# Strassen's algorithm for the output projection of a gated spatial mix, with its operand sums on GpSimd

## The chip, the core and the metric

The kernel runs on one core of a Trainium2 chip. The time is the device time of one execution in microseconds (us). The kernel before took 309.96 us (median of three runs, 309.31 to 311.14). One more execution was recorded by the hardware profiler. Names of engines: PE is TensorE (matmul), PEld its weight load, DVE VectorE, ACT ScalarE, POOL GpSimd, SP SyncE, whose queue starts nearly all DMAs here.

## The reference, cut to what matters

```python
def _B_ref(x, w_in, w_sp, b_sp, w_out):          # x: 2048 x 640
    Fh = F // 2                                  # 864
    z = _gelu(jnp.einsum('bsd,df->bsf', x, w_in))
    z1 = z[..., :Fh].copy()
    z2 = _layernorm(z[..., Fh:], axis=-1)
    g = jnp.einsum('ts,bsf->btf', w_sp, z2) + b_sp[None, :, None]    # the mix
    return jnp.einsum('bsf,fd->bsd', z1 * g, w_out)                  # the projection
...
    x = x + ga * _A_ref(h, A_k, A_v, A_shift_k, A_ssm_k, A_ssm_D)
    h = _layernorm(x, axis=-1) * (1 + cb) + sb
    x = x + gb * _B_ref(h, B_w_in, B_w_sp, B_b_sp, B_w_out)
    return x
```

Everything ahead of the mix (a long convolution by Fourier transform, layer norms, the first projection) is the same in both kernels. The change concerns the last lines: `u = z1 * g` (2048 x 864) times `w_out` (864 x 640), scaled by `gb` and added to `x`.

## The kernel before, in words

The 2048 rows are 16 tiles of 128. Tile t and tile t + 8 make pair p = t, with p from 0 to 7. The mix (2048 x 2048 times 2048 x 864) is already done by Strassen's algorithm in Winograd's form, over 2 x 2 blocks. For each pair it makes seven products, `product(p, 1)` to `product(p, 7)`. Each is 8 matmuls of 128x128 weights with 432 columns (line 1013). Its sums of `w_sp` blocks (`s_sum`, line 988) and its sums of results (`c11`, `partial`, `c22`, `last_sum`: lines 1030, 1035, 1039 to 1041, 1046 and 1047) are done by DVE. Two results are copied by ACT (`keep`, lines 1019 and 1021). The finished u of a tile is turned by a DMA on SP's queue (`turn_u`, line 1052, into the tile `uT`).

`project(t)` (line 1131) multiplies the turned tile by `w_o`, which is `w_out` times `gb`. It takes two halves of 320 output columns, each summed over seven row tiles of `w_o` (six of 128 rows and one of 96). That is 14 matmuls of 320 columns (line 1137) for a tile and 28 for a pair. DVE adds `xt` to each half (line 1139), and one DMA per tile writes the output (line 1143).

The work up to pair 0 is set by a written list. From pair 1 on a plain loop writes the order. One turn of this loop is called a pass below, and pass p makes the mix's products of pair p in the order 1, 5, 2, 6, 7, 3, 4. Tile p - 1 is projected between products 3 and 4, tile p + 7 after product 4. Pass 7 projects nothing: pairs 6 and 7 are projected behind the loop. Every engine takes its instructions in the order written. Behind product 4 SP's queue gets two loads of `w_sp` (`load_w`, line 974, in passes 1 to 4) ahead of the pair's second `turn_u`. [...]

Of the kernel before, what the change touches and what calls it, by code (L numbers as in the profile page):

```python
# [10 lines left out]
ALU = mybir.AluOpType  # L11
BF16 = mybir.dt.bfloat16
F32 = mybir.dt.float32
I32 = mybir.dt.int32

P = 128
# [19 lines left out]
SLOTS = dict(Tf=2, W=2, X=3, X1=4, KH=9, T=3, Z=3, ZT=1, wm=1, big=2, dg=2, st1=2, s1=1, sm=2, pu=2, pz=2)  # L36
# [93 lines left out]
def kernel(  # L130
# [20 lines left out]
    nc = tc.nc  # L151
    _, S, D = A_q.shape
# [3 lines left out]
    NT = S // P  # L156
    ND = D // P
    NFT = (Fh + P - 1) // P
    fsz = [min(P, Fh - i * P) for i in range(NFT)]
# [3 lines left out]
    HS = D // NH  # L163

    x_nat = A_q[0].rearrange("(n p) d -> p n d", p=P)
    out_nat = out[0].rearrange("(n p) d -> p n d", p=P)
# [9 lines left out]
    bigp = ctx.enter_context(tc.tile_pool(name="bigp", bufs=2))  # L176

    xt = persist.tile([P, NT, D], BF16)
# [14 lines left out]
    span = ctx.enter_context(tc.tile_pool(name="span", bufs=1))  # L193
# [17 lines left out]
    with ExitStack() as pctx:  # L211
# [17 lines left out]
        sums = consta.tile([P, NT, 2], F32)  # L229
# [6 lines left out]
        op = plan.op  # L236
# [549 lines left out]
        for i in range(NKC // KCH):  # L786
# [4 lines left out]
           w=["sc"])  # L791
# [165 lines left out]
        HT = NT // 2  # L957
        wTs, uTs, Ss, part, us, T = {}, {}, {}, {}, [], {}
# [13 lines left out]
        def load_w(t):  # L972
            wTs[t] = bwork.tile([P, NT, P], BF16, tag="wT", bufs=WB, name="wT")
            nc.sync.dma_start_transpose(wTs[t][:], B_w_sp[t * P:(t + 1) * P, :])

        def zb(s0, n, f):
            return tl["z2_%d" % (s0 // TB)][:, s0 % TB:s0 % TB + n, f * FC:(f + 1) * FC]

        def a_of(p, i, j):
            return wTs[p + HT * i][:, j * HT:(j + 1) * HT, :]  # L980

        def s_sum(p, k):
            if p not in Ss:
                Ss[p] = [bwork.tile([P, HT, P], BF16, tag="S%d" % i, bufs=2, name="S%d" % (i + 1)) for i in range(4)]
            S = Ss[p]
            x, y, o = ((a_of(p, 1, 0), a_of(p, 1, 1), ALU.add), (S[0][:], a_of(p, 0, 0), ALU.subtract),
                       (a_of(p, 0, 0), a_of(p, 1, 0), ALU.subtract), (a_of(p, 0, 1), S[1][:], ALU.subtract))[k]
            nc.vector.tensor_tensor(S[k][:], x, y, op=o)
# [13 lines left out]
        def product(p, m, alloc):  # L1002
            S = Ss.get(p)
            lhs = (a_of(p, 0, 0), a_of(p, 0, 1), S and S[3][:], a_of(p, 1, 1), S and S[0][:], S and S[1][:], S and S[2][:])[m - 1]
            rhs = (lambda s_: zb(s_, 1, 0), lambda s_: zb(HT + s_, 1, 0), lambda s_: zb(HT + s_, 1, 1),
                   lambda s_: T[4][:, s_:s_ + 1, :], lambda s_: T[1][:, s_:s_ + 1, :], lambda s_: T[2][:, s_:s_ + 1, :],
                   lambda s_: zb(s_, 1, 1))[m - 1]
            more = m in (2, 3, 4)
            if not more:
                part[p, BANK[m]] = alloc(BANK[m])  # L1010
            ps = part[p, BANK[m]]
            for s_ in range(HT):
                nc.tensor.matmul(ps[:, :FC], lhsT=lhs[:, s_, :], rhs=rhs(s_), start=(s_ == 0 and not more), stop=(s_ == HT - 1),  # L1013
                                 skip_group_check=more)

        def keep(p, m):
            part[p, m] = bwork.tile([P, FC], F32, tag="m%d" % m, bufs=1, name="m%d" % m)
            if m == 1:
                nc.scalar.copy(part[p, m][:], part[p, BANK[m]][:, :FC])  # L1019
            else:  # L1020
                nc.scalar.activation(part[p, m][:], part[p, BANK[m]][:, :FC], ACT.Identity, bias=T["bcol"][:, p + HT:p + HT + 1], scale=1.0)

        def f32(tag):
            return bwork.tile([P, FC], F32, tag=tag, bufs=1, name=tag)

        def ubuf(p, i):
            return us[2 * (p % 2) + i]

        def c11(p):
            nc.vector.scalar_tensor_tensor(ubuf(p, 0)[:, :FC], part[p, "a"][:, :FC], T["bcol"][:, p:p + 1], z1[p][:, :FC],  # L1030
                                           op0=ALU.add, op1=ALU.mult)

        def partial(p):
            part[p, "s"] = f32("s1")
            nc.vector.tensor_tensor(part[p, "s"][:], part[p, "b"][:, :FC], part[p, 1][:], op=ALU.add)

        def c22(p):
            c_ = f32("c22")
            nc.vector.tensor_tensor(c_[:], part[p, "c"][:, :FC], part[p, "s"][:], op=ALU.add)
            nc.vector.tensor_tensor(c_[:], c_[:], part[p, 5][:], op=ALU.add)  # L1040
            nc.vector.tensor_tensor(ubuf(p, 1)[:, FC:Fh], c_[:], z1[p + HT][:, FC:], op=ALU.mult)

        def last_sum(p, bank, i, f):
            c_, sl = f32("c"), slice(f * FC, (f + 1) * FC)
            t = p + HT * i
            nc.vector.scalar_tensor_tensor(c_[:], part[p, bank][:, :FC], T["bcol"][:, t:t + 1], part[p, "s"][:], op0=ALU.add, op1=ALU.add)
            nc.vector.tensor_tensor(ubuf(p, i)[:, sl], c_[:], z1[t][:, sl], op=ALU.mult)

        def turn_u(p, i):
            t = p + HT * i  # L1050
            uTs[t] = bwork.tile([P, NFT, P], BF16, tag="uT", bufs=UB, name="uT")
            nc.sync.dma_start_transpose(uTs[t][:], ubuf(p, i)[:])
# [33 lines left out]
        def zkeys(h, f):  # L1086
            return [("z2_%d" % h, (i, f)) for i in range(TB)]
# [3 lines left out]
        for k in (1, 2, 3, 4):  # L1091
            for h in range(2):
                lo, hi, name = h, h + 2, "T%d" % k
                r, w = {1: (zkeys(lo, 0) + zkeys(lo, 1), [("T1", h)]), 2: (zkeys(hi, 1) + [("T1", h)], [("T2", h)]),
                        3: (zkeys(hi, 1), zkeys(lo, 1)), 4: (zkeys(hi, 0) + [("T2", h)], [("T4", h)])}[k]
# [3 lines left out]
                     w=w + ([(name, "new")] if fresh else []), new=[(name, slot)] if fresh else [])  # L1099
# [5 lines left out]
        for m in (1, 5, 2, 3, 6, 7, 4):  # L1105
            b = BANK[m]
# [18 lines left out]
    psB = ctx.enter_context(tc.tile_pool(name="psB", bufs=2, space=bass.MemoryType.PSUM, reuse_waits="tile"))  # L1125
    w_o = T["w_o"]

    def bank(b):
        return psB.tile([P, 512], F32, tag="mm", bufs=6, name="ps")

    def project(t, tag="o"):
        ot = bwork.tile([P, D], BF16, tag="ot", bufs=3, name="ot")
        last = t == NT - 1
        for i, (lo, hi) in enumerate(((0, HS), (HS, HS + HS // 2), (HS + HS // 2, D)) if last else ((0, HS), (HS, D))):
            ps = psB.tile([P, 512], F32, tag=tag, bufs={"o": 2, "mm": 6}[tag], name="po")
            for ft in range(NFT):
                nc.tensor.matmul(ps[:, :hi - lo], lhsT=uTs[t][:fsz[ft], ft, :], rhs=w_o[:fsz[ft], ft, lo:hi],  # L1137
                                 start=(ft == 0), stop=(ft == NFT - 1))
            nc.vector.tensor_tensor(ot[:, lo:hi], ps[:, :hi - lo], xt[:, t, lo:hi], op=ALU.add)
            if last:  # L1140
                (nc.scalar if i == 1 else nc.sync).dma_start(out_nat[:, t, lo:hi], ot[:, lo:hi])
        if not last:
            nc.sync.dma_start(out_nat[:, t, :], ot[:])

    load_w(3)
    load_w(3 + HT)
    for p in range(1, HT):
        nxt = p + 1 < HT
        product(p, 1, bank)
        keep(p, 1)  # L1150
        product(p, 5, bank)
        keep(p, 5)
        if nxt:
            s_sum(p + 1, 0)
            s_sum(p + 1, 1)
        product(p, 2, bank)
        c11(p)
        if nxt:
            s_sum(p + 1, 2)
        product(p, 6, bank)  # L1160
        partial(p)
        product(p, 7, bank)
        c22(p)
        product(p, 3, bank)
        last_sum(p, "d", 0, 1)
        turn_u(p, 0)
        if nxt:
            project(p - 1)
        product(p, 4, bank)
        last_sum(p, "c", 1, 0)  # L1170
        if p + 3 < HT:
            load_w(p + 3)
            load_w(p + 3 + HT)
        turn_u(p, 1)
        if nxt:
            project(p - 1 + HT)
            s_sum(p + 1, 3)
    for p in range(HT - 2, HT):
        project(p, "mm")
        project(p + HT, "mm")  # L1180


# [28 lines left out]
```

## Time and profile before

| | |
|---|---|
| median of the runs | 309.96 us (309.31 to 311.14) |
| profiled execution, first to last instruction | 310.4 us |
| PE busy | 295.9 us |
| DVE busy | 254.1 us |
| ACT busy | 160.9 us |
| POOL busy | 116.0 us, none of it in the passes |
| passes 1 to 7 | 205.26 to 299.73 us |
| projection behind the loop | 299.73 to 307.56 us |

No other time of the profiled execution is given than its span, which is 0.4 us above the median of the runs. In the profile's rows the first number is a start or a stretch in us from the first instruction, the second a duration. A group row has the count, the busy time and the mean duration of one instruction. "Idle before" is the time that the engine stood still ahead of an instruction, with the engine that ended the wait behind the arrow. The matmul's own duration is longer than the distance between two matmuls, since they are pipelined. The distance is what counts, and the chain of work gives it.

### The profile page before, as it was taken

Reading aid. Unit: us, or ns where it says so; the run is one execution under the profiler, and the core shown is the slowest. Engines: PE = TensorE matmul, PEld = TensorE weight load, DVE = VectorE, ACT = ScalarE, POOL = GpSimd, SP = SyncE. Lnnn points to the kernel's source line nnn. Section 1 sums busy time; section 2 is a strip of 40 time slices with the busy share of each in tenths; the row PEclk is TensorE's granted clock in tenths of the full one; section 3 lists DMA queues with packets and bytes.
Section 4 is the critical chain, followed back from the end, with each engine's and each line's share of the span. In section 5 each row is a group of like instructions: output and inputs, shape, how many; then the busy total and the mean of one; then the engine's idle time right before and its main releaser. Section 6 shows DMA issues by size and latency. Waiting matters only on the chain.

```text
span 310.4 us, 6397 instructions
## 1 busy us (share of the span) xinstructions
PE 295.9 (95%) x2499; PEld 197.3 (64%) x2506; DVE 254.1 (82%) x515; ACT 160.9 (52%) x288; POOL 116.0 (37%) x148
## 2 busy tenths in 40 slices
PE   7897989989999998989999999999999999999996
PEld 2575778867889998645555555455565656555564
DVE  8798998979998988999895998977676858567474
ACT  6987899978888957447666687140101010010100
POOL 2531878838988999555414612000000000000000
PEclk9999999999999999999999999999999999999999
DMA  8999999998995849405698930073938284840414
GB/s 170 216 227 217 257 310 226 207 203 191 221 226 121 193 95 295 143 2 98 123 159 208 185 36 0 2 123 76 201 82 190 63 176 108 131 102 0 104 30 114
DMA packets 127953, 45.22 MB, mean 146 GB/s; under 512 B 117071, under 2 KB 127156, under 8 KB 127924
## 3 DMA queue, kind: packets, MB, share of 16 engines
q1 hardware_dynamic: 127770, 44.78, 68.3%
q8 instruction: 19, 0.31, 0.4%
q14 instruction: 10, 0.08, 0.1%
q10 hardware_dynamic: 154, 0.05, 0.1%
HBM read 16.11 MB, written 5.24 MB: 69 GB/s over the span
## 4 chain that ended last, share of the span: by engine, by line
PE 37%; DVE 19%; POOL 2%; DMA 2%; issue 1%; ACT 1%; POOLq 1%; DVEq 0%; SPq 0%
PE ps L1013 23%; PE po L1137 10%; DVE stz L926 4%; DVE st L704 3%; DMA Z<-Z 2%; PE pz L1013 1%; DVE Tf L462 1%; PE pu L245 1%; DVE xt L698 1%; DVE X L943 1%; POOL rstd L191 1%; DVE T L998 1%; DVE T L462 1%; DVE mv L829 1%; DVE gh L746 1%
## 5 line engine op out<-in xcount | busy, mean ns | idle before, releaser
L245 PEld LDWEIGHTS <-Z 128*128 128x128 bf16 x320 | 31.2, 98 | 28.0 <-DVE Z L871 1.3
L245 PE MATMUL pu<-X,M 128*128 128x128 bf16 (+1 forms) x480 | 45.7, 237 | 2.5 <-DVE Tf L462 2.1
L245 PEld LDWEIGHTS <-M 128*128 128x128 bf16 x480 | 37.3, 98 | 8.7 <-issue 3.1
L1019 ACT COPY m<-ps 128x432 f32<-128x432 f32 x7 | 3.6, 518 | 72.7 <-PE ps L1013 72.7
L1013 PEld LDWEIGHTS <-S 128*128 128x128 bf16 x256 | 25.0, 98 | 22.9 <-issue 1.3
L476 POOL TENSOR_TENSOR W<-Tf 128x256 bf16<-128x256 f32 x47 | 34.7, 760 | 11.4 <-DVE Tf L462 8.1
L245 PE MATMUL pz<-big,Z 128*128 128x432 bf16 x160 | 33.1, 346 | 0.8 <-DVE Z L871 0.8
L248 ACT CAST X<-s 128x1024 bf16<-128x1024 f32 x31 | 31.9, 1030 | 3.1 <-PE s L245 2.9
L1137 PE MATMUL po<-w_o,uT 128*128 128x320 bf16 (+2 forms) x231 | 32.7, 295 | 0.0
L245 PE MATMUL pu<-big,Z 128*128 128x432 bf16 x160 | 32.5, 346 | 0.0
L462 DVE TENSOR_TENSOR Tf<-pu,KH 128x1024 f32<-128x1024 f32 x25 | 30.3, 1219 | 2.6 <-POOL gh L608 1.1
L1013 PEld LDWEIGHTS <-wT 128*128 128x128 bf16 x192 | 18.7, 98 | 15.2
L1137 PEld LDWEIGHTS <-uT 128*128 128x128 bf16 (+1 forms) x231 | 22.2, 98 | 9.7
L245 PEld LDWEIGHTS <-G 128*128 128x128 bf16 x330 | 24.7, 98 | 2.3 <-issue 0.5
L248 ACT CAST KH<-pu 128x512 bf16<-128x512 f32 x40 | 23.0, 600 | 5.9 <-PE pu L245 5.8
L248 ACT CAST Z<-pz 128x512 bf16<-128x512 f32 x38 | 22.3, 602 | 5.3 <-PE pz L245 5.1
L1013 PE MATMUL ps<-T,S 128*128 128x432 bf16 x112 | 22.7, 346 | 0.0
L1013 PE MATMUL ps<-X,wT 128*128 128x432 bf16 x112 | 22.7, 346 | 0.0
L245 PEld LDWEIGHTS <-X 128*128 128x128 bf16 x288 | 18.1, 97 | 6.4 <-DMA X<-kv_scr 1.6
L1013 PE MATMUL ps<-X,S 128*128 128x432 bf16 x112 | 21.6, 346 | 0.0
L245 PE MATMUL s<-F1bd,X 128*128 128x256 bf16 x128 | 19.2, 272 | 1.5 <-DVE X L400 1.2
L245 PE MATMUL sm<-big,dg 128*128 128x512 bf16 (+3 forms) x73 | 19.9, 379 | 0.5
(181 smaller groups left out, 542.6 us busy)
## 6 DMA issues: line engine op xcount, KB each, us to landing
wm<-in_w_mod_dram SPq DMA_DIRECT2D x6, 800.0 KB, 6.2
xt<-in_A_q_dram SPq DMA_DIRECT2D x4, 640.0 KB, 6.2
out_dram<-ot SPq DMA_DIRECT2D x15, 160.0 KB, 2.1
big<-in_B_w_in_dram SPq DMA_DIRECT2D x2, 1080.0 KB, 9.5
X<-in_A_ssm_k_dram SPq DMA_DIRECT2D x4, 512.0 KB, 5.2
kv_scr<-big SPq DMA_DIRECT2D x4, 512.0 KB, 3.5
X<-kv_scr SPq DMA_DIRECT2D x4, 512.0 KB, 4.7
w_o<-in_B_w_out_dram SPq DMA_DIRECT2D x6, 160.0 KB, 3.1
```

What stands on the lines that cost most here:

```text
L191: nc.gpsimd.tensor_tensor(dst, dst, mhalf[:, 0:dst.shape[1]], op=ALU.pow)
L245: nc.tensor.matmul(o, lhsT=w, rhs=x, start=start, stop=stop)
L248: (e.copy if e is nc.scalar else e.tensor_copy)(dst, src)
L462: e.tensor_tensor(T_[:], (tl[pu] if src is None else tl[src])[:, :, :, None, :].to_broadcast(shape), tl[KH][:, :, None, :, :].to_broadcast ...
L476: e.tensor_tensor(tl[W][:, :, o, :], T_[:, :, 0, o, :], T_[:, :, 1, 1 - o, :], op=ALU.add if o else ALU.subtract)
L698: op("GD" if u < NU - 1 else "D", "res", lambda e: e.tensor_tensor(sl, sl, gl, op=ALU.add), r=[("gh", (u, g))], w=[("xt", (u, n)) for n in ...
L704: op("D", "ln2", lambda e, n=n: e.bn_stats(out=st2[:, n, (0, 0, 0, 1, 2)[u], :], in_=xt[:, n, us[0] * DU:(u + 1) * DU]), r=[("xt", (v, n)) ...
L746: op("D", "yml", lambda e, ghv=ghv, py=py, i0=i0, k=k: e.tensor_tensor(ghv, ghv, tl[py][:, i0:i0 + k], op=ALU.mult), r=[py], w=[("gh", (u, ...
L926: op("D", "stz", lambda e, i=i, n=n, fc=fc: e.bn_stats(out=stz[:, n, fc, :], in_=tl[z2][:, i, fc * FC:(fc + 1) * FC]), r=[(z2, (i, fc))], ...
L1013: nc.tensor.matmul(ps[:, :FC], lhsT=lhs[:, s_, :], rhs=rhs(s_), start=(s_ == 0 and not more), stop=(s_ == HT - 1), skip_group_check=more)
L1019: nc.scalar.copy(part[p, m][:], part[p, BANK[m]][:, :FC])
L1137: nc.tensor.matmul(ps[:, :hi - lo], lhsT=uTs[t][:fsz[ft], ft, :], rhs=w_o[:fsz[ft], ft, lo:hi], start=(ft == 0), stop=(ft == NFT - 1))
```

## The change

The projection of pairs 0 to 6 is done by Strassen's algorithm too (Winograd's form). The blocks are the two tiles of a pair by two groups of three row tiles of `w_o`, and the two halves of 320 columns. Seven products of 3 matmuls take the place of eight. The seventh row tile of `w_o` (96 rows) is left over, and is multiplied in the plain way by 4 further matmuls. So a pair has 25 matmuls of 320 columns. Pair 7 is projected as before.

- `weight_sum` makes four sums of `w_o` blocks once (960 columns each; two on POOL, two on DVE) and a fifth small one on POOL (`V5`).
- `u_sums(p)` makes four sums of the turned tiles of a pair on POOL (384 columns each). They wait for both turned tiles.
- `begin` (6 matmuls) stands between products 3 and 4, `most` (15 matmuls) behind product 4, and `end` (4 matmuls) behind product 5 of the next pass.
- Two results per pair are copied by ACT (lines 1197 and 1199). DVE makes five additions with a PSUM operand (lines 1204, 1210, 1217, 1219, 1224) in place of four. POOL makes four additions of 320 columns per pair in SBUF (lines 1200 and 1205 to 1207).
- The banks are 4 for the mix and 4 for the projection. `vbuf`, `rbuf` and `obuf` lie in slots of earlier tiles.

The core of the diff:

```diff
     def bank(b):
-        return psB.tile([P, 512], F32, tag="mm", bufs=6, name="ps")
+        return psB.tile([P, 512], F32, tag="mm", bufs=4, name="ps")
+
+    def obank():
+        return psB.tile([P, 512], F32, tag="o", bufs=4, name="po")
...
+    def weight_sum(e, k):
+        x, y = ((wo_b(0, 1), wo_b(0, 0)), (wo_b(1, 1), V[0]), (wo_b(1, 1), wo_b(0, 1)), (wo_b(1, 0), V[1]))[k]
+        e.tensor_tensor(V[k], x, y, op=ALU.subtract)
...
+    def u_sums(p):
+        R = [rbuf[:, p % 2, i] for i in range(4)]
+        lo, hi = p, p + HT
+        for k, (x, y, o) in enumerate(((u_of(hi, 0), u_of(hi, 1), ALU.add), (R[0], u_of(lo, 0), ALU.subtract),
+                                       (u_of(lo, 0), u_of(hi, 0), ALU.subtract), (u_of(lo, 1), R[1], ALU.subtract))):
+            nc.gpsimd.tensor_tensor(R[k], x, y, op=o)
+        return R
...
+        def begin():
+            piece(a, U[0, 0], B[0, 0], KT, True, True)
+            nc.scalar.copy(m1, a[:, :HS])
+            piece(d, S_[0], V_[0], KT, True, True)
+            nc.scalar.copy(m5, d[:, :HS])
+            nc.gpsimd.tensor_tensor(m5, m5, x_of(1, 1), op=ALU.add)
+
+        def most():
+            piece(b, S_[1], V_[1], KT, True, True)
+            nc.vector.tensor_tensor(s, b[:, :HS], m1, op=ALU.add)
+            nc.gpsimd.tensor_tensor(s12, s, x_of(0, 1), op=ALU.add)
+            nc.gpsimd.tensor_tensor(s22, s, m5, op=ALU.add)
+            nc.gpsimd.tensor_tensor(s21, s, x_of(1, 0), op=ALU.add)
+            piece(a, U[0, 1], B[1, 0], KT, False, False)
+            piece(a, *rest(lo, 0), False, True)
+            nc.vector.tensor_tensor(ot[0][:, 0:HS], a[:, :HS], x_of(0, 0), op=ALU.add)
+            piece(c_, S_[2], V_[2], KT, True, False)
+            piece(c_, *rest(hi, 1), False, True)
+            piece(d, S_[3], B[1, 1], KT, False, False)
+            piece(d, *rest(lo, 1), False, True)
+
+        def sums():
+            nc.vector.tensor_tensor(ot[0][:, HS:D], d[:, :HS], s12, op=ALU.add)
+            nc.sync.dma_start(out_nat[:, lo, :], ot[0][:])
+            nc.vector.tensor_tensor(ot[1][:, HS:D], c_[:, :HS], s22, op=ALU.add)
+
+        def end():
+            piece(c_, U[1, 1], V_[3], KT, False, False)
+            piece(c_, lambda k: uTs[hi][:fl, NFT - 1, :], lambda k: V5[:fl, :], 1, False, True)
+            nc.vector.tensor_tensor(ot[1][:, 0:HS], c_[:, :HS], s21, op=ALU.add)
+            nc.sync.dma_start(out_nat[:, hi, :], ot[1][:])
+        return begin, most, sums, end
+
     load_w(3)
     load_w(3 + HT)
+    weight_sum(nc.gpsimd, 2)
+    weight_sum(nc.vector, 0)
+    R = u_sums(0)
+    weight_sum(nc.vector, 1)
+    weight_sum(nc.gpsimd, 3)
+    nc.gpsimd.tensor_tensor(V5[:fl, :], w_o[:fl, NFT - 1, 0:HS], w_o[:fl, NFT - 1, HS:D], op=ALU.subtract)
+    end = None
     for p in range(1, HT):
         nxt = p + 1 < HT
         product(p, 1, bank)
         keep(p, 1)
         product(p, 5, bank)
         keep(p, 5)
+        if end:
+            end()
...
         c22(p)
+        begin, most, sums, end = project_pair(p - 1, R)
         product(p, 3, bank)
         last_sum(p, "d", 0, 1)
         turn_u(p, 0)
-        if nxt:
-            project(p - 1)
+        begin()
         product(p, 4, bank)
...
         turn_u(p, 1)
+        most()
         if nxt:
-            project(p - 1 + HT)
             s_sum(p + 1, 3)
-    for p in range(HT - 2, HT):
-        project(p, "mm")
-        project(p + HT, "mm")
+        sums()
+        if nxt:
+            R = u_sums(p)
+    project(HT - 1)
+    end()
+    project(NT - 1)
```

DVE's queue in pass 3, from the last operation on product 3's result to the end of the pass. `S` are the sums of `s_sum`, `u` the finished mix, `ot` the output tile. Before:

```order
L1047 TENSOR_TENSOR u_2790<-c,M_80 128x432
L1139 TENSOR_TENSOR ot<-po,xt 128x320 x2
L1046 SCALAR_TENSOR_TENSOR c<-ps,bcol,s_3737 128x432
L1047 TENSOR_TENSOR u_2791<-c,G_81 128x432
L1139 TENSOR_TENSOR ot<-po,xt 128x320 x2
L988 TENSOR_TENSOR S_3715<-wT,S_3713 128x1024
```

With the change (`O` is `obuf`, the additions' other operand, written by ACT, DVE and POOL):

```order
L1047 TENSOR_TENSOR u_2790<-c,M_80 128x432
L1046 SCALAR_TENSOR_TENSOR c<-ps,bcol,s_3765 128x432
L1047 TENSOR_TENSOR u_2791<-c,G_81 128x432
L1204 TENSOR_TENSOR O<-po,O 128x320
L1210 TENSOR_TENSOR ot<-po,xt 128x320
L988 TENSOR_TENSOR S_3743<-wT,S_3741 128x1024
L1217 TENSOR_TENSOR ot<-po,O 128x320
L1219 TENSOR_TENSOR ot<-po,O 128x320
```

The four output additions, which stood behind the two tiles' matmuls, are now five and all stand behind product 4's sums. L1217 and L1219 take operands that POOL makes from the result of L1204, and everything of the next pass stands behind them.

POOL's queue from the start of pass 1, where it had nothing (`V` are the sums of `w_o`, `R` those of the turned tiles):

```order
L1161 TENSOR_TENSOR V<-w_o 128x960
L1171 TENSOR_TENSOR R<-uT 128x384
L1171 TENSOR_TENSOR R<-R,uT 128x384
L1171 TENSOR_TENSOR R<-uT 128x384
L1171 TENSOR_TENSOR R<-uT,R 128x384
L1161 TENSOR_TENSOR V<-w_o,V 128x960
L1235 TENSOR_TENSOR V<-w_o 96x320
L1200 TENSOR_TENSOR O<-O,xt 128x320
L1205 TENSOR_TENSOR O<-O,xt 128x320
L1206 TENSOR_TENSOR O<-O 128x320
L1207 TENSOR_TENSOR O<-O,xt 128x320
```

All three `V` sums stand ahead of the first pair's L1200. For the later pairs the four `R` and the four `O` sums alternate.

More of the change, by code (lines that the diff above doesn't have):

```diff
@@ L1128, in bank, with project @@
     def bank(b):
-        return psB.tile([P, 512], F32, tag="mm", bufs=6, name="ps")
-    def project(t, tag="o"):
+        return psB.tile([P, 512], F32, tag="mm", bufs=4, name="ps")
+    def obank():
+        return psB.tile([P, 512], F32, tag="o", bufs=4, name="po")
+    def project(t):
         ot = bwork.tile([P, D], BF16, tag="ot", bufs=3, name="ot")
@@ L1134, in project @@
         for i, (lo, hi) in enumerate(((0, HS), (HS, HS + HS // 2), (HS + HS // 2, D)) if last else ((0, HS), (HS, D))):
-            ps = psB.tile([P, 512], F32, tag=tag, bufs={"o": 2, "mm": 6}[tag], name="po")
+            ps = obank()
             for ft in range(NFT):
@@ L1143, in project, with wo_b @@
             nc.sync.dma_start(out_nat[:, t, :], ot[:])
+    KT = NFT // 2
+    fl = fsz[-1]
+    vbuf = bigp.tile([P, (4 * KT + 1) * HS], BF16, tag="big", bufs=SLOTS["big"], name="V")
+    V = [vbuf[:, i * KT * HS:(i + 1) * KT * HS].rearrange("p (k d) -> p k d", d=HS) for i in range(4)]
+    V5 = vbuf[:, 4 * KT * HS:]
+    rbuf = span.tile([P, 2, 4, KT, P], BF16, tag="Z", bufs=SLOTS["Z"], name="R")
+    obuf = span.tile([P, 6, HS], F32, tag="Z", bufs=SLOTS["Z"], name="O")
+    def wo_b(i, j):
+        return w_o[:, i * KT:(i + 1) * KT, j * HS:(j + 1) * HS]
@@ new lines, in weight_sum, with u_of @@
+    def weight_sum(e, k):
+        x, y = ((wo_b(0, 1), wo_b(0, 0)), (wo_b(1, 1), V[0]), (wo_b(1, 1), wo_b(0, 1)), (wo_b(1, 0), V[1]))[k]
+        e.tensor_tensor(V[k], x, y, op=ALU.subtract)
+    def u_of(t, i):
+        return uTs[t][:, i * KT:(i + 1) * KT, :]
+    def u_sums(p):
[5 more added lines that the diff above has]
+        return R
@@ new lines, in rows, with piece, project_pair, rest @@
+    def rows(i):
+        return obuf[:, i]
+    def piece(ps, w, x, n, start, stop, m=P):
+        for k in range(n):
+            nc.tensor.matmul(ps[:, :HS], lhsT=w(k), rhs=x(k), start=start and k == 0, stop=stop and k == n - 1, skip_group_check=True)
+    def project_pair(p, R):
+        lo, hi = p, p + HT
+        U = {(i, j): (lambda k, t=t, j=j: uTs[t][:, j * KT + k, :]) for i, t in ((0, lo), (1, hi)) for j in range(2)}
+        B = {(i, j): (lambda k, i=i, j=j: w_o[:, i * KT + k, j * HS:(j + 1) * HS]) for i in range(2) for j in range(2)}
+        S_ = [lambda k, i=i: R[i][:, k, :] for i in range(4)]
+        V_ = [lambda k, i=i: V[i][:, k, :] for i in range(4)]
+        def rest(t, j):
+            return (lambda k: uTs[t][:fl, NFT - 1, :]), (lambda k: w_o[:fl, NFT - 1, j * HS:(j + 1) * HS]), 1
+        ot = [bwork.tile([P, D], BF16, tag="ot", bufs=3, name="ot") for _ in range(2)]
+        x_of = lambda i, j: xt[:, (lo, hi)[i], j * HS:(j + 1) * HS]
+        m1, m5, s, s12, s21, s22 = (rows(i) for i in range(6))
+        a, d, b, c_ = (obank() for _ in range(4))
+        def begin():
[27 more added lines that the diff above has]
+        return begin, most, sums, end
```

## The prediction

> **What bounds the kernel now.** I read the totals first, then a table of engine time by stretch, then the chain that ended last, then DVE's and the DMA queue's order of time in one pass. The totals, and two stretches of about a pass each (length, busy time and instructions of PE, PEld, DVE, ACT and POOL, the clock, DMA):
>
> ```profile
> PE 295.9 (95%) x2499; PEld 197.3 (64%) x2506; DVE 254.1 (82%) x515; ACT 160.9 (52%) x288; POOL 116.0 (37%) x148
> ...
> 232.00:246.00 14.00, 14.00 (x86) 8.19 (x84) 9.70 (x18) 1.14 (x2) 0.00 (x0) 1.00 0.60 130
> 260.00:274.00 14.00, 14.00 (x86) 8.16 (x85) 9.70 (x18) 1.14 (x2) 0.00 (x0) 1.00 0.72 132
> ```
>
> PE never rests in a pass, at full clock. DVE has 4.3 of 14 us free, ACT nearly all, POOL does nothing. The end of the chain of waits (start, us, what):
>
> ```profile
> 270.35 1.91 PE po L1137 x14
> 272.26 1.46 PE ps L1013 x8
> 273.72 1.91 PE po L1137 x14
> 275.63 8.76 PE ps L1013 x48
> ...
> 289.67 10.22 PE ps L1013 x56
> 299.89 7.67 PE po L1137 x63
> 307.56 0.02 issue
> ```
>
> A mix matmul takes 10.22 / 56 = 0.1825 us, a projection matmul 1.91 / 14 = 0.1364, and a pass 289.67 - 275.63 = 14.04 = 10.22 + 28 x 0.1364. Only PE's count, or a new wait of PE, moves the end.
>
> **What is removed.** Three matmuls per pair, seven pairs: 21 x 0.1364 = **-2.86 us**. The matmuls keep their shape, so they keep their price. An undisturbed pass becomes 10.22 + 25 x 0.1364 = 13.63 us.
>
> **The tail loses cover: +0.55.** The start of product 4 of pass 7, the first turn of pair 7 on SP's queue, and what its DMAs take to land (least, median, most):
>
> ```profile
> 298.27 1.62 PE L1013 MATMUL ps<-T,wT 128*128 128x432 bf16 x8
> ...
> 300.25 2.64 SPq L1052 DMA_TRANSPOSE uT<-u  x2
> ...
> DMA to landing us min/median/max: 2.9/2.9/4.7
> ```
>
> From the end of product 3 (298.27) to the turned tile 7 it is 300.25 + 2.9 - 298.27 = 4.88 us. Before, product 4 and two tiles cover this (1.46 + 28 x 0.1364 = 5.28). Now it is `begin`, product 4 and `most`: 0.82 + 1.46 + 2.05 = 4.33. PE waits 0.55, or 2.35 if this landing is one of the slow ones. Tile 15 needs 1.5 (below) + 2.9 = 4.4 us from the end of product 4 and has `most`, the wait, tile 7 and `end`, 2.05 + 0.55 + 1.91 + 0.55 = 5.06, so it is not late.
>
> **What DVE, ACT and POOL get.** Prices of POOL, DVE and ACT (the first three with least, median and most in ns; then busy us and mean ns):
>
> ```profile
> L476 POOL TENSOR_TENSOR W<-Tf x47: 721/727/967, 29.7 to 120.3; 128x256 bf16<-128x256 f32 x47
> L698 POOL TENSOR_TENSOR xt<-xt,gh x10: 1145/1152/1395, 86.4 to 142.7; 128x512 bf16<-128x512 bf16 x10
> L988 DVE TENSOR_TENSOR S<-wT x16: 629/682/687, 155.1 to 280.6; 128x1024 bf16<-128x1024 bf16 x16
> ...
> L1047 DVE TENSOR_TENSOR u<-c,G 128x432 bf16<-128x432 f32 x9 | 5.5, 608 | 0.3
> L1139 DVE TENSOR_TENSOR ot<-po,xt 128x320 bf16<-128x320 f32 x30 | 14.0, 486 | 3.0 <-PE po L1137 3.0
> L1019 ACT COPY m<-ps 128x432 f32<-128x432 f32 x7 | 3.6, 518 | 72.7 <-PE ps L1013 72.7
> ```
>
> By columns, an `R` sum on POOL (384, bf16) is 1.152 x 384 / 512 = 0.87 us. An `O` sum (320, float) lies between 1.152 x 320 / 512 = 0.72 and 0.727 x 320 / 256 = 0.91. I take 0.9, from the float row. The big `V` sums are 2.17 on POOL and, between DVE's rows, 0.65 on DVE. ACT's two copies (0.4 each) hide in its 12.9 idle us. DVE's fifth addition (0.49) hides in its 4.3 us. The smaller banks cost nothing while DVE keeps within a pass: each is filled once a pass, and its reader runs within 3 us of the product.
>
> POOL's 4 x 0.87 + 4 x 0.9 = 7.1 us a pass would fit too. What speaks against it is how the two engines meet in earlier stages (DVE with POOL, four meetings):
>
> ```profile
> 86.52 1.12 DVE L400 TENSOR_TENSOR X<-X,D_col 128x16 bf16<-128x16 bf16 x1
> 86.39 1.16 POOL L698 TENSOR_TENSOR xt<-xt,gh 128x512 bf16<-128x512 bf16 x1
> ...
> 136.98 0.83 DVE L833 SCALAR_TENSOR_TENSOR nmr<-mv,rstd 128x2 f32<-128x2 f32 x1
> 136.63 1.15 POOL L698 TENSOR_TENSOR xt<-xt,gh 128x512 bf16<-128x512 bf16 x1
> ...
> 125.44 0.42 DVE L698 TENSOR_TENSOR xt<-xt,gh 128x512 bf16<-128x512 bf16 x1
> 125.48 1.40 POOL L698 TENSOR_TENSOR xt<-xt,gh 128x512 bf16<-128x512 bf16 x1 [0.84 <-DVE gh L678]
> ...
> 103.50 1.21 DVE L462 TENSOR_TENSOR T<-pu,KH 128x1024 bf16<-128x1024 f32 x1
> 103.67 1.15 POOL L698 TENSOR_TENSOR xt<-xt,gh 128x512 bf16<-128x512 bf16 x1
> ```
>
> Two tiny DVE operations that start inside a POOL sum end only with it (86.52 + 1.12 = 87.64 against 87.55). In the third, POOL starts second and takes 1.40 in place of 1.15: it ends 1.15 - 0.13 after DVE. In the fourth DVE has one operand in PSUM, and neither is slower. So a DVE operation with both operands in SBUF and a POOL sum **exclude each other**, and the later costs its full length less about 0.14. In a pass eight DVE operations are of this kind: four `s_sum`, L1040, L1041 and two L1047, 4 x 0.68 + 4 x 0.61 = 5.2 us. With POOL's 7.1 that is 12.3 of 13.63 us, in orders fixed by hand.
>
> [...]
>
> **Where PE meets this: `end`.** It adds to the bank that L1219 reads, so it waits for L1219, and that for POOL's second `O` sum. Behind `end` on PE stands the whole pass. *Later pairs.* A row of DVE for what follows product 4, whose last matmul ended at 273.56, and SP's queue in a pass with loads, product 4 ended at 217.39:
>
> ```profile
> 273.76 0.67 DVE L1046 SCALAR_TENSOR_TENSOR c<-ps,bcol,s 128x432 f32<-128x432 f32 x1 [0.85 <-PE ps L1013]
> ...
> 217.39 2.07 PE L1137 MATMUL po<-w_o,uT 128*128 128x320 bf16 x14
> ...
> 217.92 5.10 SPq L974 DMA_TRANSPOSE wT<-in_B_w_sp_dram  x2
> 223.11 1.25 SPq L1052 DMA_TRANSPOSE uT<-u  x1
> ```
>
> From the end of product 4, with DVE punctual: L1046 and L1047 until 1.5, L1204 2.0, POOL's first `O` sum 3.0, DVE's `s_sum` held by it until 3.55, POOL's second `O` sum held by that until 4.3, L1219 until 4.9. PE wants `end` after `most` and two products, 2.05 + 2.92 = 4.97. That is just in time. But DVE is not punctual: the second turned tile lands 223.11 + 2.9 - 217.39 = 8.6 us after product 4 (10.4 at worst), so the four `R` sums, 3.5 us plus waits of 0.5 each, run until 13.6 to 15.5 us. They fall on L1040, L1041 and L1047 of the next pass, each held by up to 0.7, where about 0.5 us is spare ahead of the next L1046. DVE comes 0 to 1.2 us late. A wait in one pass gives the next that much more room. I take 0.35 for each of five pairs: **+1.75** (0 to 3.5).
>
> *The first pair* has POOL's `V` sums ahead too. The start of pass 1, and the scaling of `w_o` on which they wait:
>
> ```profile
> 204.91 1.69 DVE L1077 TENSOR_TENSOR w_o<-w_o,gb_bf 128x640 bf16<-128x640 bf16 x4
> 205.26 1.62 PE L1013 MATMUL ps<-X,wT 128*128 128x432 bf16 x8
> ```
>
> Counted from 205.26, POOL begins at 1.3. Until the second `O` sum it has 2 x 2.17 + 4 x 0.87 + 0.7 + 3 x 0.9 = 11.2 us, done at 12.5 alone. DVE's ten operations of the kind in this time (two `V`, four `s_sum`, four float) each push it by their length less 0.14: 1.3 + 2.7 + 2.4 - 1.4 = 5.0. Done at 17.5, L1219 at 18.1. PE wants `end` at 10.22 + 21 x 0.1364 + 2.92 = 16.0. The wait is 2.1, or none without exclusion, or 3.5 where POOL also waits for DVE's other work. I take **+2.4**.
>
> **Sum:** -2.86 + 0.55 + 1.75 + 2.4 = +1.84 us. On the profiled span, 310.4 becomes 312.2. The median of the runs lies 0.4 below that span: 311.8.
>
> **Rivals.** A measurement here can tell about 0.5% (1.55 us) from no change: under 308.4 is faster, over 311.5 slower.
> - *The sums stay out of PE's way* (17%). DVE and POOL interleave with less loss, L1219 is on time, only the tail waits: 309.96 - 2.86 + 0.55 = 307.7. For it: the slack computed above, and the undisturbed meetings with PSUM operands. Against: the three held meetings.
> - *Only the 16-bit sums exclude* (15%). In the first pair the push falls to 1.3 + 2.7 - 0.8 = 3.2 us, so L1219 ends at 16.3 and the wait is 0.3 to 0.9; later pairs are in time: 309.96 - 2.86 + 0.55 + 0.6 = 308.3 (308.0 to 308.6), on the edge of faster. For it: two of the three held meetings are of 16-bit operands. Against: L833 is not.
> - *SP's queue spreads the delay* (15%), slower still. A late L1047 delays a `turn_u`, behind it in SP's queue the loads (5.1 us), behind them the second turn; then `begin` waits for the `R` sums too. It decides from a landing 8.8 us into a pass (9.7, when `begin` reaches `R`, less one sum), where 6.6 is usual and 8.4 the worst by the rows above. With 1 us for each of the four passes with loads: 315.8.
>
> **Numbers.** The forecast has 53%, of which two thirds lie over 311.5 and the rest within 0.5%. Slower: 0.37 + 0.15 = 0.52. Faster: nearly all of the first rival and half of the second, 0.22. Same: 0.26. The range runs from the first rival, 307.7, to my upper waits, -2.86 + 0.9 + 3.5 + 3.5 = +5.0: 315.0. The forecast alone would be 310.5 to 314.
>
> **What would show it.** Passes: waits of PE behind product 5 (at `end`), released by DVE L1219, largest in pass 2, about half a microsecond in some later passes. `s_sum` and L1040 to L1047 above 0.68 and 0.61 us, POOL sums above 0.9. At product 4 of pass 7 a wait of 0.55 for the turned tile. If PE has no gap before `end`, exclusion does not reach it and the kernel is faster; if gaps stand at `begin`, SP's queue was the cause. A pass of 13.63 us without a gap would show that the removed matmuls were worth their price.

## The result, and the profile after

The changed kernel is slower: 313.36 us against 310.17 us (medians of 14 runs each). The ratio is 1.0085, with a 95% interval of 1.0056 to 1.0113, so about +2.6 us (1.7 to 3.5). One run of the changed kernel, at 316.03 us, counts as slow and is left out of the ratio. The medians lie 3.2 us apart, which is inside the interval. The profiled execution spans 312.4 us, 2.0 more than before. Its pass 1 begins 0.68 us earlier than in the profile before (204.58 against 205.26). The work ahead of pass 1 is the same and scatters by more than that between profiles: in the run with pair 0 in the plain way, where pass 2 began at 217.47, pass 1 began at about 203.4, by an estimate from an undisturbed pass of 14.04 us. So everything below is counted from the start of pass 1.

The totals of the page of the changed kernel, and two stretches (length, busy time and instructions of PE, PEld, DVE, ACT and POOL, the clock, DMA):

```profile
PE 295.8 (95%) x2485; PEld 195.7 (63%) x2485; DVE 271.5 (87%) x524; ACT 167.1 (53%) x302; POOL 177.1 (57%) x207
...
218.00:233.00 15.00, 12.87 (x77) 7.22 (x74) 12.55 (x20) 1.99 (x4) 7.13 (x7) 1.00 0.65 124
263.00:277.00 14.00, 14.00 (x85) 8.13 (x84) 11.74 (x19) 1.99 (x4) 8.13 (x9) 1.00 0.54 115
```

PE, which had no idle time in the stretches of the prediction, is now idle for 2.1 us in the first of these two. DVE's busy time rose from 9.70 us in a stretch of 14 to 11.74 in 14 and 12.55 in 15, though in a pass it got only one operation of 0.49 us more. The waits of PE, in total (us in total, how often, the longest):

```profile
PE po L1179 <- DVE ot L1219: 2.8, 2, 2.1
PE po L1179 <- POOL R L1171: 1.1, 1, 1.1
PE po L1140 <- DMA uT<-u: 0.5, 1, 0.5
```

Below a wait is taken from the starts of matmuls: the distance between two starts, less the usual 0.1825 or 0.1364 us per matmul. This also finds the small waits, and does not depend on the modelled ends. In the changed kernel the waits are, in us:

| place | pass 2 | pass 3 | pass 4 | passes 6, 7 and behind | sum |
|---|---|---|---|---|---|
| `end`, for DVE L1219 | 2.29 | 0.80 | | 0.11 and 0.11 | 3.31 |
| last `R` sum, in `most` | 0.24 | | | | 0.24 |
| first `R` sum, in `begin` | | | 1.29 | | 1.29 |
| behind the loop, tile 7 | | | | 0.67 | 0.67 |
| all | | | | | 5.51 |

In the kernel before there is none of these. -2.86 us for the removed matmuls and 5.51 of waits give +2.65 us, which is what the runs show. In the profiles, from the first matmul of pass 1 to the last matmul of all, it is 104.73 us against 102.05, +2.68.

The largest wait, in order of time (start, duration), from the end of product 4 of pass 1 to `end` in pass 2:

```profile
215.62 0.57 PE L1179 MATMUL po<-V,R 128*128 128x320 bf16 x3
...
219.13 1.62 PE L1013 MATMUL ps<-T,S 128*128 128x432 bf16 x8
219.15 0.61 DVE L1047 TENSOR_TENSOR u<-c,G 128x432 bf16<-128x432 f32 x1
...
219.68 0.48 DVE L1204 TENSOR_TENSOR O<-po,O 128x320 f32<-128x320 f32 x1
...
220.24 0.80 POOL L1205 TENSOR_TENSOR O<-O,xt 128x320 f32<-128x320 f32 x1 [2.47 <-DVE O L1204]
220.47 1.11 DVE L988 TENSOR_TENSOR S<-wT,S 128x1024 bf16<-128x1024 bf16 x1
...
220.99 1.32 POOL L1206 TENSOR_TENSOR O<-O 128x320 f32<-128x320 f32 x1
...
222.34 0.49 DVE L1219 TENSOR_TENSOR ot<-po,O 128x320 bf16<-128x320 f32 x1 [0.35 <-POOL O L1206]
222.88 0.70 PE L1179 MATMUL po<-V,uT 128*128 128x320 bf16 x4 [2.13 <-DVE ot L1219]
```

Product 4 ended at 215.62, where the next projection matmul starts. A punctual DVE begins the product's last sum (L1047) about 0.9 us later, at 216.5. It began at 219.15, 2.6 us late. Behind it come L1204, POOL's first `O` sum, `s_sum` held by that sum (1.11 in place of 0.68), the second `O` sum held by `s_sum` (1.32 in place of 0.79), and L1219. What had made DVE late stands earlier in pass 1:

```profile
206.05 2.29 POOL L1161 TENSOR_TENSOR V<-w_o 128x960 bf16<-128x960 bf16 x1 [16.57 <-DVE w_o L1077]
...
206.52 2.34 DVE L1161 TENSOR_TENSOR V<-w_o,V 128x960 bf16<-128x960 bf16 x1
...
208.78 1.40 DVE L988 TENSOR_TENSOR S<-wT 128x1024 bf16<-128x1024 bf16 x1
...
213.55 2.00 POOL L1161 TENSOR_TENSOR V<-w_o,V 128x960 bf16<-128x960 bf16 x1
...
214.15 1.86 DVE L1040 TENSOR_TENSOR c<-c,m 128x432 f32<-128x432 f32 x1
```

DVE's second `V` sum took 2.34 in place of 0.65, and the first two `s_sum` 1.40 and 1.28 in place of 0.68, beside POOL's `V` and `R` sums. At the start of L1039 (213.44) DVE was 1.4 us late by this. Then a float addition of 0.61 us took 1.86, and ended 0.46 after POOL's sum. That is its length less 0.15. L1041 behind it took 1.08. These holds make 3.1 us, of which about 0.5 were spare ahead of the next operation. The groups of DVE, from 204 us on, the means in ns:

```profile
L988 DVE TENSOR_TENSOR S<-wT,S 128x1024 bf16<-128x1024 bf16 x7 | 7.4, 1060 | 0.0
L1041 DVE TENSOR_TENSOR u<-c,G 128x432 bf16<-128x432 f32 x7 | 6.5, 929 | 0.2
L1040 DVE TENSOR_TENSOR c<-c,m 128x432 f32<-128x432 f32 x7 | 6.4, 909 | 0.7
...
L1039 DVE TENSOR_TENSOR c<-ps,s 128x432 f32<-128x432 f32 x7 | 4.3, 608 | 3.4 <-PE ps L1013 3.1
```

L1040 and L1041 have both operands in SBUF and took 0.91 and 0.93 in place of 0.61. L1039, of the same size but with one operand in PSUM, kept 0.608.

### The profile page after: what moved, and what is told of

Same layout as the page of the kernel before. It is cut to its first block, busy times and chain, and to the rows that moved or that the text cites. A ratio compares the mean times of both kernels' runs of the same rounds, so it can differ in the third digit from the quotient of the medians.

```text
span 312.4 us, 6505 instructions
## 1 busy us (share of the span) xinstructions
PE 295.8 (95%) x2485; PEld 195.7 (63%) x2485; DVE 271.5 (87%) x524; ACT 167.1 (53%) x302; POOL 177.1 (57%) x207
## 4 chain that ended last, share of the span: by engine, by line
PE 45%; DVE 8%; POOL 4%; issue 3%; DMA 2%; ACT 1%; DVEq 0%; POOLq 0%
PE ps L1013 17%; PE pu L245 9%; PE pz L245 9%; PE po L1179 6%; DMA uT<-u 2%; POOL R L1171 2%; PE pz L1013 1%; PE po L1140 1%; DVE Tf L462 1%; DVE T L462 1%; POOL O L1206 1%; DVE st L704 1%; PE pu L1013 1%; DVE xt L698 1%; DVE T L998 1%
## 5 line engine op out<-in xcount | busy, mean ns | idle before, releaser
L476 POOL TENSOR_TENSOR W<-Tf 128x256 bf16<-128x256 f32 x47 | 34.8, 761 | 12.3 <-DVE Tf L462 8.4
L245 PE MATMUL pu<-big,Z 128*128 128x432 bf16 x160 | 33.5, 354 | 0.0
L1197 ACT COPY O<-po 128x320 f32<-128x320 f32 x7 | 3.0, 426 | 46.0 <-PE po L1179 46.0
L1171 POOL TENSOR_TENSOR R<-uT 128x384 bf16<-128x384 bf16 x14 | 14.8, 1055 | 19.8 <-DMA uT<-u 19.8
L245 PE MATMUL sm<-big,dg 128*128 128x512 bf16 (+1 forms) x80 | 20.4, 379 | 0.0
```

The lines of the kernel that those rows point to most:

```text
L245: nc.tensor.matmul(o, lhsT=w, rhs=x, start=start, stop=stop)
L476: e.tensor_tensor(tl[W][:, :, o, :], T_[:, :, 0, o, :], T_[:, :, 1, 1 - o, :], op=ALU.add if o else ALU.subtract)
L1171: nc.gpsimd.tensor_tensor(R[k], x, y, op=o)
```

## Experiments

The first theory is that of the prediction: DVE's operations on two SBUF operands and POOL's sums exclude each other, and what is late then shows on PE at `end`, or, by way of SP's queue, at `begin`. Its rivals are that POOL's chain is simply long, that only the place of `end` is at fault, and that POOL's work slows the core in another way. All ratios are to the kernel before. The edits are made to the changed kernel, but for the idle sums, which are put into the kernel before.

### `end` later, the second turn earlier, and both

The edit of the first, `end` behind product 6:

```diff
         keep(p, 5)
-        if end:
-            end()
...
         partial(p)
+        if end:
+            end()
         product(p, 7, bank)
```

> Edit: the four matmuls of `end` and DVE's L1224 stand behind product 6 of the next pass in place of product 5, 2.9 us later. Theory (VectorE and GpSimd exclude each other, and the lateness that this leaves in the passes runs on into SP's queue): the waits of PE at `end` (3.3 us in the changed kernel) go, but the room that they gave the next pass goes too, so the wait at `begin` for the R sums grows from 1.3 us to 2 to 3, in an earlier pass; with 0.7 at the tail 310.2 - 2.86 + 3.2 = 310.5 (310 to 311.5). Rival (only the place of `end` is at fault): nothing else grows, 1.3 + 0.2 + 0.7 us of waits are left, 309.5.

The edit of the second, the pair's second turn ahead of the loads in SP's queue:

```diff
+        turn_u(p, 1)
         if p + 3 < HT:
             load_w(p + 3)
             load_w(p + 3 + HT)
-        turn_u(p, 1)
         most()
```

> Edit: the second turn of a pair stands ahead of the two loads of w_sp in SP's queue, nothing else. Theory (the waits at `begin` come from SP's queue, those at `end` from the exclusion): `begin` and the R sums no longer wait (1.3 + 0.2 us gone), `end` of the first pair still waits 2 to 2.7 us, the later ones 0 to 0.9, the tail 0.7: 310.2 - 2.86 + 3.8 = 311.1 (310.5 to 312). Rival (the R sums are late because GpSimd is slow, not because their input is): the wait at `begin` stays, 312.8.

The third has both edits.

> Edit: `end` behind product 6 and the second turn ahead of the loads, both together. Theory: each step has room for what the exclusion costs, all waits but the tail's 0.6 go, and the removed matmuls are worth their 2.86 us: 308.0 (307.5 to 309). Rival (the loss is in the shape of the work, in banks, copies or matmul prices): the passes stay longer than 13.63 us and the time stays over 309.5.

| | waits of PE, us | -2.86 + waits, us | measured ratio |
|---|---|---|---|
| the changed kernel | 5.51 | +2.65 | 1.0085 (1.0056 to 1.0113) |
| `end` later | 3.57 | +0.71 | 1.0042 (1.0011 to 1.0072) |
| turn earlier | 3.33 | +0.47 | 1.0026 (0.9999 to 1.0052) |
| both | 0.68 | -2.18 | 0.9940 (0.9914 to 0.9966) |

PE's largest wait with `end` later, then with the turn earlier, and all of PE's waits with both (total, times, longest):

```profile
229.69 0.58 PE L1179 MATMUL po<-V,R 128*128 128x320 bf16 x3 [2.23 <-POOL R L1171]
```
```profile
223.01 0.70 PE L1179 MATMUL po<-V,uT 128*128 128x320 bf16 x4 [2.13 <-DVE ot L1219]
```
```profile
PE po L1140 <- DMA uT<-u: 0.5, 1, 0.5
```

With `end` later every wait at `end` went, and the one at `begin` grew from 1.29 to 2.40 + 0.48 us and came two passes earlier. So the lateness was not used up: in the changed kernel PE's wait at `end` had given SP's queue the time it needed. The rival that only the place of `end` is at fault expected 1.3 us there, and 2.88 were measured. With the turn earlier the waits at `begin` went and the first `end` kept its 2.30 us. By the waits either edit alone gives back about 2 us, both together 4.8. On 310.2 us, from which the expectations were reckoned, the three ratios make 311.5, 311.0 and 308.3 us; the first is at the upper end of its range. With both, all passes run without a gap and only the tail waits. The removed matmuls are then worth what was reckoned, and the banks, copies and shapes of the change cost nothing that shows.

DVE is still slowed in that kernel: the three `s_sum` groups take 900 to 1184 ns, where the changed kernel has 858 to 1060, and L1040 and L1041 take 788 and 675, where it has 909 and 929. Exclusion is still there, and only its way to PE is cut.

### POOL busy, but not with sums

In two runs each of POOL's sums in the passes is replaced by a power of a few columns that takes about as long. The sums are left out, while order and waits stay. The edit for `R` and one `O` sum stands here, and the others are alike. The first filled `R` and `V` by DMA:

```diff
-            nc.gpsimd.tensor_tensor(R[k], x, y, op=o)
+            nc.gpsimd.tensor_tensor(R[k][:, 0, 0:3], ones[:, 0:3], (x if k in (0, 2) else y)[:, 0, 0:3], op=ALU.pow)
...
-            nc.gpsimd.tensor_tensor(m5, m5, x_of(1, 1), op=ALU.add)
+            nc.gpsimd.tensor_tensor(m5[:, 0:2], ones[:, 0:2], m5[:, 0:2], op=ALU.pow)
```

> Edit: the changed kernel with every sum of GpSimd in the passes (V, R and O) replaced by a power of 2, 3 or 10 columns that takes about as long (in the kernel before a power of 2 to 8 columns took 0.7 to 1.7 us, and VectorE's operations beside one kept their length). The sums are left out, R and V are filled once from w_sp by DMA and O by a copy; order and waits stay. Theory (exclusion): VectorE's s_sum and L1040 to L1047 keep 0.68 and 0.61 us, `end` waits under 0.5 us in all, 0.7 at the tail, 0 to 1 at `begin`: 308.0 to 309. Rival (GpSimd's chain is just long): the first pair waits about as long at `end` as in the changed kernel, 1.5 to 2.5 us, 310.5 or more.

The ratio was 0.9970 (0.9943 to 0.9996), and 1.07 us were left at the first `end`, more than the theory allowed. But the filling DMAs had made POOL start 3 us late and stand still for 2.6 us more, so this run does not tell the theories apart on that point. The second let DVE do the filling:

> Edit: as the run with powers in place of GpSimd's sums, but V and R are filled with zeros by VectorE, since the filling DMAs had made GpSimd start 3 us late and wait 2.6 us more. The sums are left out as there. Theory (exclusion): GpSimd is as busy as in the changed kernel, VectorE keeps 0.68 and 0.61 us, and PE waits nowhere but at the tail (0.7) and at most 0.5 at `begin`: ratio to before 0.994 (0.992 to 0.997). Rival (the length of GpSimd's chain makes the first pair wait): 1 us or more is left at `end` of the first pair, 0.998 or more.

The ratio was 0.9928 (0.9899 to 0.9958). PE waited 0.46 us once at `begin` and 0.67 at the tail, and nowhere at `end`. Groups of DVE (L990 is `s_sum` here, L1042 and L1043 are L1040 and L1041) and of POOL, means in ns:

```profile
L1042 DVE TENSOR_TENSOR c<-c,m 128x432 f32<-128x432 f32 x7 | 4.3, 609 | 0.7
L1043 DVE TENSOR_TENSOR u<-c,G 128x432 bf16<-128x432 f32 x7 | 4.2, 607 | 0.2
L990 DVE TENSOR_TENSOR S<-wT,S 128x1024 bf16<-128x1024 bf16 x6 | 4.1, 681 | 0.0
```
```profile
L1176 POOL TENSOR_TENSOR R<-ones,uT 128x3 bf16<-128x3 f32 x21 | 19.2, 938 | 23.4 <-DMA uT<-u 17.5 <-PE ps L1015 6.0
L1210 POOL TENSOR_TENSOR O<-ones,O 128x2 f32<-128x2 f32 x7 | 4.9, 696 | 9.3 <-DVE O L1209 9.3
```

POOL's chain is nearly as long as that of undisturbed sums (0.94 against 0.91 for an `R` sum, 0.70 against 0.79 for an `O` sum), stands in the same order and releases the same operations. For the first pair its first `O` power ended 12.8 us after the start of pass 1, where the changed kernel's first `O` sum ended after 13.2. DVE's two float sums have their own lengths back to the nanosecond (609 and 607), its `s_sum` groups to within 7 ns (676 to 691 against 682 to 692), and the waits at `end` are gone. So the length of POOL's chain by itself was not the cause. What cost the time is that POOL's sums and DVE's operations hold each other up. In what way they do so, no run here shows: the powers differ from the sums in the operation and in the columns that they move. The float sums L1040 and L1041 are held as the 16-bit ones are (0.91 and 0.93 us in the changed kernel, 0.61 here).

### Pair 0 in the plain way

```diff
-        begin, most, sums, end = project_pair(p - 1, R)
+        if p > 1:
+            begin, most, sums, end = project_pair(p - 1, R)
...
-        begin()
+        if p > 1:
+            begin()
+        else:
+            project(0)
...
```

In the same way `project(HT)` takes the place of the first `most`, and pair 0 has no `R` sums and no `sums`.

> Edit: the changed kernel with pair 0 projected in the plain way, so that the sums of w_o have a whole pass before the first product that needs them. It gives back 3 matmuls, 0.41 us. Theory: the wait of 2.3 us at the first `end` came from these sums in front of the pair's own, so it goes and no other of its size comes; the later waits stay between 0.5 and 2.5 us, the tail 0.7: -2.45 + 0.7 + 1.5 = -0.3, ratio 0.999 (0.996 to 1.003). Rival (any first pair waits so): 2 us at the first `end`, ratio 1.006 or more.

The ratio was 1.0025 (0.9999 to 1.0052), at the upper end of what was expected. The waits sum up to 3.45 us (-2.45 + 3.45 = +1.0). The 2.3 us at the first `end` are gone, and no wait of that size came: 1.15 at the `begin` of pair 1, 1.6 in all at `end` and in `most` (0.79 the longest), 0.68 at the tail. So the first pair's wait was due to the `V` sums in front of its own. The wait at `begin` is again SP's queue's: there the two loads held the queue for 4.8 us ahead of the second turn.

### The kernel before, with idle sums on POOL

```diff
             project(p - 1 + HT)
             s_sum(p + 1, 3)
+            u_sums(p)
+            o_sums(p)
```

POOL makes four `R` and four `O` sums ahead of pass 1 and in each of passes 1 to 6, and two `V` sums ahead, and nobody reads them.

> Edit: the kernel before, with GpSimd making the sums V[2], V[3], R and O in every pass (two R buffers, the four O sums right behind the four R sums) whose results nobody reads. Theory (exclusion costs only where PE waits for its result): VectorE's s_sum and L1040 to L1047 grow by 0.1 to 0.4 us on average, PE has no gap, since before there is room, and the time is the same: ratio 1.000 (0.997 to 1.003). Rival (GpSimd's work itself slows the core, by its memory traffic or its clock): passes over 14.1 us, ratio 1.005 or more.

The ratio was 1.0072 (1.0048 to 1.0096), slower, which the theory had not expected. PE's waits:

```profile
PE po L1137 <- DVE ot L1139: 1.2, 1, 1.2
PE po L1137 <- DMA uT<-u: 0.3, 1, 0.3
```

By the starts they are 1.33, 0.22 and 0.42 at the tail, 1.97 us in all, nearly the whole loss of 2.2. So the rival's reason does not hold either: between the waits the matmuls keep their distance. Its largest wait, in order of time:

```profile
212.88 2.36 POOL L1172 TENSOR_TENSOR V<-w_o,V 128x960 bf16<-128x960 bf16 x1
...
213.42 2.29 DVE L1041 TENSOR_TENSOR u<-c,G 128x432 bf16<-128x432 f32 x1
...
215.24 1.62 PE L1013 MATMUL ps<-T,wT 128*128 128x432 bf16 x8
...
216.32 1.25 DVE L1047 TENSOR_TENSOR u<-c,M 128x432 bf16<-128x432 f32 x1
...
217.50 0.88 DVE L1139 TENSOR_TENSOR ot<-po,xt 128x320 bf16<-128x320 f32 x2
218.03 1.25 PE L1137 MATMUL po<-w_o,uT 128*128 128x320 bf16 x8 [1.17 <-DVE ot L1139]
```

DVE is held twice, its output addition comes late, and the bank that it reads is one of only two that the kernel before has for the projection. PE wanted it at 215.24 + 8 x 0.1825 = 216.70 and got it at 218.03. So the exclusion reaches PE even where nothing that POOL makes is used.

### A version that is faster than both kernels

Both edits, and in the last pass product 3 ahead of product 7:

```diff
+        if nxt:
+            product(p, 7, bank)
+            c22(p)
         product(p, 3, bank)
         last_sum(p, "d", 0, 1)
         turn_u(p, 0)
+        if not nxt:
+            product(p, 7, bank)
+            c22(p)
         begin()
```

> Edit: `end` behind product 6 and the second turn ahead of the loads, and in the last pass product 3 stands ahead of product 7, so that tile 7 is turned 1.5 us earlier against PE. Theory (the tail's wait is the turned tile): no wait of PE is left in the passes or behind them, 0.6 us less than with the two edits alone: ratio 0.992 (0.990 to 0.994). Rival (the turned tile 15 is late in its place, its cover shrinks to 4.5 us where it needs 4.4): a wait of 0.3 or more before the last tile, 0.994.

The ratio was 0.9901 (0.9865 to 0.9938), 3 us faster than before. The tail's wait for tile 7 is gone. A wait of 0.22 us is left before the last `end`, and none for tile 15. The gain over the version without the third edit agrees with its 0.46 us less of waits, but the two intervals overlap, so this last step is shown by the waits alone.

## Why the prediction was right

- **The removed matmuls** were worth 2.86 us. In the changed kernel -2.86 + 5.51 is the measured loss, and with both edits the passes run gapless.
- **The tail**: 0.55 forecast, 0.67 measured (0.67 to 0.69 in the other runs with this order). The rows of the changed kernel, SP's turns and PE's first matmul of tile 7:

```profile
302.07 3.00 SPq L1052 DMA_TRANSPOSE uT<-u  x2
...
304.99 2.08 PE L1140 MATMUL po<-w_o,uT 128*128 128x320 bf16 x14 [0.51 <-DMA uT<-u]
```

- **The first pair**: 2.4 forecast, 2.29 measured, released by L1219 as named. The second `O` sum ended 17.7 us after the start of pass 1 (17.5 forecast). The way there was another, so the close agreement is in part luck: the prediction had POOL busy without a pause until then, but POOL stood still for 2.47 us ahead of its first sum behind L1204, because DVE, held by POOL's earlier sums, came 2.6 us late with the result. That the `V` sums made it is shown by the run with pair 0 in the plain way; that exclusion and not the length of POOL's chain made it, by the run with powers.
- **The later pairs**: 1.75 forecast, all of it at `end`; measured 1.02 at `end`, 0.24 for the last `R` sum and 1.29 at `begin`, 2.55 in all. This term was too small by 0.8 us, and half of what was measured stood in the place that the third rival named. That rival was to decide from a turned tile that lands 8.8 us into a pass. In pass 4, which began at 248.27, the `R` sum could start at 258.30, 10.0 us into it. SP's queue, POOL and PE there:

```profile
247.97 6.77 SPq L974 DMA_TRANSPOSE wT<-in_B_w_sp_dram  x2
254.82 1.30 SPq L1052 DMA_TRANSPOSE uT<-u  x1
...
258.30 0.91 POOL L1171 TENSOR_TENSOR R<-uT 128x384 bf16<-128x384 bf16 x1 [7.10 <-DMA uT<-u]
...
259.27 0.58 PE L1179 MATMUL po<-V,R 128*128 128x320 bf16 x3 [1.12 <-POOL R L1171]
```

The two loads held the queue for 6.77 us, where the prediction had 5.1. With 5.1 the `R` sum could have started at 256.6, by this estimate, and PE, which came to it at 257.98, would not have waited. So this wait came by SP's queue, but it needed the slow loads: the late L1047 that the rival had in mind would not have made it alone. What made them slow is open. One of the two took 4.65 us, and a packet of the instruction queue began with it, at 247.9. But the kernel before has such a packet too, at 246.6, in a load of usual length (2.68), and no run tried it. The rival had 1 us in each of four passes; it came in one, since in pass 2 the wait at `end` gave the queue its time, as the run with `end` later shows.

- **The prices**: undisturbed, an `R` sum took 0.91 us (0.87 forecast) and an `O` sum 0.79 (0.9). POOL's second `O` sum was held by `s_sum` in six of seven pairs (mean 1.25 over all), as the chain of the prediction had it.
- **The sum** was +1.84 and came out as +2.65 by the waits. The difference is the later pairs' term. The direction and the main path were right; that size was not.
- **The first rival** (the sums stay out of PE's way, 307.7) did not happen, but the order with both edits comes near its time (0.9940 of 309.96 is 308.1). **The second** (only the 16-bit sums exclude) fails by the groups L1040 and L1041. It set the 16-bit sums apart from the float sums, but the runs show both held (`s_sum` took 0.86 to 1.06 us in place of 0.68).

## What to carry to other kernels

Work moved to an idle GpSimd was not free for VectorE here: its float sums on two SBUF operands took 0.91 and 0.93 us on average in place of 0.61, `s_sum` 0.86 to 1.06 in place of 0.68, and GpSimd's second `O` sum 1.25 in place of 0.79. So for such a plan each VectorE operation on two SBUF operands and each GpSimd sum are best added up as if they ran on one engine, and their sum set against the pass. When the sum nearly fills the pass, as 12.3 of 13.6 us did here by the prediction's prices, the order decides: the ratio was 1.0085 without the two edits and 0.9940 with them. A step that waits for the result belongs one or two products later, and the transfers that feed GpSimd belong ahead of loads that nobody waits for soon. An edit that removes one wait may only move it, so look for the next one in the same chain before it is judged.

## What was not expected of the hardware

Sums on GpSimd that nobody reads made the kernel before 0.72% slower (1.0048 to 1.0096). The largest of the three waits of the matmuls (1.33 us) and the one at the tail (0.42) follow VectorE additions that were held: one of 0.61 us took 2.29 us beside a GpSimd sum of 960 columns, and the wait at the tail follows one of 1.15 us, behind which the turn of tile 7 started late. Powers on GpSimd, of two to ten columns and 0.7 to 0.9 us each for the most part, left VectorE's sums of 432 columns at 0.607 to 0.609 us and `s_sum` at 0.68 to 0.69. So it was not GpSimd being busy that held VectorE up, but the kind of work it did.
